# Second layer of a two-layer network on one core: all engines in source order, and the tile border reordered

## The chip, the cores and the metric

The kernel runs on 1 core of one Trainium2 chip. The metric is the device time of one execution in microseconds (us). The engines are named as in the profile: PE (TensorE), PEld (its weight loads), DVE (VectorE), ACT (ScalarE), POOL (GpSimd), SP (SyncE, which here only issues DMAs).

## The reference

An mLSTM-like attention over 4 batches, 8 heads, 768 steps and head size 40 gives 3072 tokens of 320 numbers. Two feed-forward layers follow, each 320 -> 2048 -> 320:

```
x  = attention(q, k, v, gates)             # 3072 x 320
x1 = square(max(x  @ w_in1, 0)) @ w_out1   # layer 0 in the code
h  = x1 @ w_in2                            # layer 1 in the code
g  = where(h > 0, h, exp(min(h, 0)) - 1)
out = g @ w_out2
```

All of it is float32. On PE each float32 operand is split into a high part (fp32r) and a rest, and three products high*high, high*low, low*high are added.

## The kernel before

Tokens are cut into 6 tiles of 512 (`NTILE`, `TT`), the hidden size of 2048 into 16 blocks of 128 (`NF`). `steps` lists (layer l, tile j, block m), step `k` being its index; the loop at L815 goes through them. The attention and the first steps are written out by hand (`ORDER`); the attention of later tiles is woven into the steps of layer 0. This change is about the second layer, l = 1, and the last two steps ahead of it.

In the second layer two blocks go together, so work is done at even `k`. `first_pair(k)` makes the hidden values of blocks m and m+1: 15 "slots" of two matmuls each, one on the lower 64 rows of the array and one on the upper 64 rows, into two PSUM tiles `h`. `elem(k)` and `elem(k+1)` make g from them: ACT `r` = relu(-h) (L520), `th` = tanh(r/2) (L521), `ex` = exp(-r) (L522); DVE two `scalar_tensor_tensor` (L523, L524); POOL the rounded `ghi` (L525). `elem_lo` is the rest `glo` on DVE (L530). `second_half(k)` multiplies half of the pair's rows into the four PSUM accumulators `acc0` to `acc3` (four groups of 128 tokens): 48 matmuls of 320 columns are needed for a pair, 24 in a first pass and 24 in a second pass ("again") with lower and upper rows exchanged. After a first pass `pass_banks` has ACT read one number of the accumulator written last into `mark` (the tile `room`, L615); the second pass waits for it.

The order on PE in the second layer is that of the source: in the step of pair k first `first_pair(k+2)`, then `second_half(k-2)` (second pass), then `second_half(k)` (first pass). So the elementwise work of a pair has the second passes and the first products of the next pair to hide behind.

At the border between tiles (m == 0, j > 0) the second pass of the old tile's last pair is followed by `put` (L626), which copies the four accumulators to SBUF (L639 on DVE) and stores them (L642 on SP). The copies go through `yp`, tag `y`, which has 3 buffers (`yp = pool("y", bufs=3)`, L86), so a fourth copy needs the buffer of the first. The new tile's `second_half(k)` then begins in the same four accumulators, one buffer each; at a border the passes work on `acc0` with `acc2` first, then on `acc1` with `acc3`.

PE alone has its source order there (`manual_schedule(engines={pe.engine})`, L819). ACT, DVE, POOL and SP are put in order by the scheduler of the framework, which estimates when each instruction will be ready. `behind(e)` only says that an instruction comes after the engine's last one traced so far.

Two side jobs run in the same loop. `y_split` (L653) cuts the next tile's input, read back from DRAM by `y_load`, into high and low parts, one of five slices at m = 2, 4, 6, 8, 10: ACT `hi` (L668), DVE `lo` (L669), and for the last slice (m = 10, c = 4) first a DVE addition `yr` (L667). In the source it stands ahead of the step's `pass_banks`. `w_next` prepares the second layer's weights block by block (L868 to L875): ACT `w_top` (L130) and `w_low` (L135), DVE `w_add` (L140), POOL `w_hi` (L144), DVE `w_lo` (L150). These steps run in the last tile of layer 0 and at even m of the second layer's first tile until 16 blocks are done.

Of the kernel before, what the change touches and what calls it, by code (L numbers as in the profile page):

```python
# [27 lines left out]
NF = DFF // 128  # L28
# [5 lines left out]
NTILE = NT // TT  # L34
# [29 lines left out]
def body(tc, qk, qp, kvo, gates, wq, ident_in, qkm_in, out):  # L64
    nc = tc.nc
    pe, act, dve, pool_, sp = nc.tensor, nc.scalar, nc.vector, nc.gpsimd, nc.sync
    es = ExitStack()

    def pool(name, bufs=1, stack=es, **kw):
        return stack.enter_context(tc.tile_pool(name=name, bufs=bufs, **kw))  # L70
# [372 lines left out]
    def attn_pe(t):  # L443
        u, k = divmod(t, 4)
        if k == 0:
            units(u, lambda u: [f() for f in scores(2 * u)])
        elif k == 1:
            units(u - 1, lambda w: [f() for f in trans(w)])
            units(u, lambda u: [f() for f in scores(2 * u + 1)])
        for c in range(1, NCH):  # L450
            if t == (16 * c - 9 if c > 1 else 9):
                for f in gate_cols(c):
                    f()
# [24 lines left out]
    def turn(t):  # L478
        for f in (attn_pre, attn_pe, attn_mul, attn_post, attn_last):
            f(t)  # L480

    G, HB, ACC = {}, {}, {}
# [45 lines left out]
    def elem_lo(k):  # L528
        hi, lo, r = G[k]
        dve.tensor_tensor(out=lo, in0=r, in1=hi.bitcast(F32), op=ALU.subtract)  # L530

    def acc_tile(i):
        return (pacc if i < 3 else bp["a"]).tile([128, 512], F32, tag=f"acc{i}", name=f"acc{i}")
# [34 lines left out]
    def first_pair(k):  # L568

        l, j, m, _ = steps[k]  # L570
        w = W[l, m]
        hi, lo = X[NTILE + j]
        ops = []
        for c in range(5):
            ws, wlo = (w[:, o + c * 128:o + c * 128 + 128] for o in (0, WC))
            ops += [(ws, hi[c]), (ws, lo[c]), (wlo, hi[c])]
        for i, t in enumerate((ph, bp["h"])):
            HB[k + i] = t.tile([128, TT], F32, tag="h", name="h")
        for n, (a, b_) in enumerate(ops):
            for i, r in enumerate((LOW, HIGH)):  # L580
                pe.matmul(HB[k + i], lhsT=a[r], rhs=b_[r], start=n == 0, stop=n == len(ops) - 1)  # L581

    def second_ops(k, i):

        l, j, m, _ = steps[k]
        w, cs, ops = W[l, m + 1], slice(i * L, (i + 1) * L), []
        for x in range(2):
            hi, lo, _ = G[k + x]
            wh, wl = (w[:, o + 384 * x:o + 384 * x + DM] for o in (0, WC))
            ops += [(hi[:, cs], wh), (hi[:, cs], wl), (lo[:, cs], wh)]  # L590
        return ops
# [4 lines left out]
    def second_half(k):  # L596

        l, j, m, _ = steps[k]
        if (l, j) not in ACC:
            ACC[l, j] = [acc_tile(i) for i in range(4)]  # L600
        again = k in begun
        begun.add(k)
        parts = [range(6)] if again else [(0, 1, 3, 4), (2, 5)]
        todo = []
        for own, r in zip(banks, (LOW, HIGH)):
            ops = {i: second_ops(k, i) for i in own}
            todo.append([(i, ops[i][n][0][r], ops[i][n][1][r], n) for part in parts for i in own for n in part])
        for pair in zip(*todo):
            for i, a, b_, n in pair:
                pe.matmul(ACC[l, j][i][:, 0:DM], lhsT=a, rhs=b_, start=m == 0 and not again and n == 0, stop=n == 5 and (not again or m + 2 == NF), skip_group_check=m > 0 or again)  # L610
# [15 lines left out]
    def put(k):  # L626
        l, j, m, _ = steps[k]
        if m < NF - 1:
            return
        for i, a in enumerate(ACC.pop((l, j))):  # L630
            if l == 0:
                t = yp.tile([128, TT], F32, tag="y", name="y")
                act.activation(out=t, in_=a, func=AF.Copy)
                sp.dma_start(out=y_dr[i, :, j * TT:(j + 1) * TT], in_=t)
            else:
                last = j == NTILE - 1
                t = (bp["t"].tile([128, TT], F32, tag="th", name="yl") if last and i == 3 else yp.tile([128, TT], F32, tag="y", name="y"))[:, 0:DM]
                if not last or i % 2:
                    dve.tensor_copy(t, a[:, 0:DM])  # L639
                else:  # L640
                    act.activation(out=t, in_=a[:, 0:DM], func=AF.Copy)
                (act if last and i % 2 else sp).dma_start(out=out[j * 4 + i], in_=t)  # L642
# [159 lines left out]
    def first(k):  # L802
        nonlocal nm
        todo = []
        while nm <= min(k, len(steps) - 1):
            for f in mm1(nm):
                f()
            todo.append(nm)
            nm += 1
        return todo  # L810

    def behind(e):
        return tc.issue_after(next(i for i in reversed(nc.cur_bb.bb.instructions) if i.engine == e.engine))

    for k in range(NK, len(steps)):  # L815
        l, j, m, _ = steps[k]
        if k == (NTILE - 1) * NF:
            early.close()
            es.enter_context(tc.manual_schedule(engines={pe.engine}))  # L819
            for e in (act, dve, pool_, sp):  # L820
                es.enter_context(behind(e))
        last = l == 0 and j == NTILE - 1
        ts = []
        if l == 0 and j + 1 < NTILE:
            to = 16 * j + m + 22
            ts = list(range(nt, min(TEND, to)))
            nt += len(ts)
        if last and m == 0:
            ea.close()
            bp["y"] = pool("by", reuse_waits="tile")  # L830
            bp["x"] = pool("bx", reuse_waits="tile")
            bp["t"] = pool("bt", bufs=2, reuse_waits="tile")
            bp["g"] = pool("bg", bufs=2, reuse_waits="tile")
            bp["a"] = pool("pa", space=PSUM, reuse_waits="tile")
            bp["h"] = pool("pb", bufs=2, space=PSUM, reuse_waits="tile")
        for t in ts[:-1]:
            turn(t)
        for t in ts[-1:]:
            attn_pre(t)
        if l or last and m > 13:  # L840
            todo = []
            if k % 2 == 0 and k + 2 < len(steps):
                first_pair(k + 2)
                todo = [k + 2, k + 3]
        else:
            todo = first(k + 2)
        for t in ts[-1:]:
            attn_pe(t)
        if l and j and m == 0:
            second_half(k - 2)  # L850
            put(k - 1)
        for e in todo:
            elem(e)
        for t in ts[-1:]:
            attn_mul(t)
        for e in todo:
            elem_lo(e)
        for t in ts[-1:]:
            attn_post(t)
        if l == 0 and j == 1 and 3 < m < 7:  # L860
            w_next(0, w_load)
        if l == 0 and 1 < j < NTILE - 1:
            if m == 5:
                w_next(1, w_top, w_low)
            if m == 8:
                w_next(2, w_add)
                w_next(0, w_load)
        if last or l == 1 and j == 0 and m % 2 == 0:  # L868
            if w_n[3] < min(w_n[2], NF + m if last else 2 * NF):
                w_next(3, w_hi, w_lo)  # L870
            if w_n[1] < min(w_n[0], NF + m if last else 2 * NF):
                w_next(1, w_top, w_low)
                w_next(2, w_add)
            if w_n[0] < min(w_n[2] + 3, 2 * NF):
                w_next(0, w_load)  # L875
        jn = j + 1 if l else 0
        if (l or last) and jn < NTILE:
            if m == 13 and jn + 1 < NTILE or last and m == 1:
                y_load(jn + (m > 1))
            if m in (2, 4, 6, 8, 10) if l else m in (4, 6, 8, 10, 12):  # L880
                with behind(act), behind(dve):
                    y_split(jn, (m - 2) // 2 if l else (m - 4) // 2)
        if l:
            if k % 2 == 0:
                if m and k < len(steps) - 2:
                    second_half(k - 2)
                if k < len(steps) - 4:
                    second_half(k)
                    pass_banks(j)
                elif k == len(steps) - 4:  # L890
                    second_whole(k)
            if k == len(steps) - 1:
                second_whole(k - 1)
                put(k)
            continue
        for f in mm2(k):
            f()
        put(k)
        for t in ts[-1:]:
            attn_last(t)  # L900
# [70 lines left out]
```

## Time and profile before

| | us |
|---|---|
| median of 3 runs | 840.22 |
| lowest, highest | 839.46, 840.56 |
| the profiled execution, its own time | 839.09 |
| its span, first to last instruction | 837.3 |
| PE busy | 802.4 |
| DVE busy | 531.9 |
| ACT busy | 513.4 |
| POOL busy | 158.0 |
| mean granted PE clock | 0.984 |

The profile is of one execution. The second layer's first products start at 454.77 us of the span and its last copy ends at 834.39 us. PE is busy nearly throughout, so what can be gained or lost lies in the short stretches where it waits or where its granted clock (1.0 is 2.4 GHz, 0.5 is 1.2 GHz) is low.

### The profile page before, as it was taken

Reading aid. Unit: us, or ns where it says so; the run is one execution under the profiler, and the core shown is the slowest. Engines: PE = TensorE matmul, PEld = TensorE weight load, DVE = VectorE, ACT = ScalarE, POOL = GpSimd, SP = SyncE. Lnnn points to the kernel's source line nnn. Section 1 sums busy time; section 2 is a strip of 40 time slices with the busy share of each in tenths; the row PEclk is TensorE's granted clock in tenths of the full one; section 3 lists DMA queues with packets and bytes.
Section 4 is the critical chain, followed back from the end, with each engine's and each line's share of the span. In section 5 each row is a group of like instructions: output and inputs, shape, how many; then the busy total and the mean of one; then the engine's idle time right before and its main releaser. Section 6 shows DMA issues by size and latency. Waiting matters only on the chain.

```text
span 837.3 us, 17781 instructions
## 1 busy us (share of the span) xinstructions
PE 802.4 (96%) x7058; PEld 701.3 (84%) x7058; DVE 531.9 (64%) x956; ACT 513.4 (61%) x1018; POOL 158.0 (19%) x209
## 2 busy tenths in 40 slices
PE   8999999999999999999999999898899799799798
PEld 5688788888888888888888898898898798798798
DVE  5899976866567665543486766565466466466454
ACT  5799776777768667774897655454354354354343
POOL 3233210100100000100122322122122122122121
PEclk9999999999999999999999999999899899999899
DMA  9997455757454455613256103003003003000000
GB/s 228 311 296 224 123 159 124 250 137 179 138 154 148 110 163 145 185 52 77 106 186 167 38 2 77 32 2 77 32 2 77 32 2 76 33 1 2 32 2 32
DMA packets 33257, 88.22 MB, mean 105 GB/s; under 512 B 3735, under 2 KB 7319, under 8 KB 33175
## 3 DMA queue, kind: packets, MB, share of 16 engines
q1 hardware_dynamic: 32887, 86.77, 37.1%
q8 instruction: 55, 0.90, 0.5%
q10 hardware_dynamic: 288, 0.33, 0.1%
q14 instruction: 27, 0.22, 0.1%
HBM read 78.35 MB, written 8.73 MB: 104 GB/s over the span
## 4 chain that ended last, share of the span: by engine, by line
PE 74%; DVE 12%; ACT 4%; DMA 4%; issue 4%; POOL 2%; SPq 1%; POOLq 0%; ACTq 0%; DVEq 0%
PE h L581 18%; PE acc L610 17%; PE acc L546 15%; PE h L501 15%; DVE w L150 2%; DVE ct L140 2%; PE pv L331 2%; DMA mb<-negm_dr 2%; DVE ex L523 2%; PE s L320 1%; PE in L331 1%; DVE glo L530 1%; DMA kvo<-kvo 1%; ACT ct L135 1%; DVE r L524 1%
## 5 line engine op out<-in xcount | busy, mean ns | idle before, releaser
L530 DVE TENSOR_TENSOR glo<-r,ghi 128x512 fp32r<-128x512 f32 x192 | 133.3, 695 | 111.3 <-ACT r L516 88.2
L501 PE MATMUL h<-xh,w 128*128 128x512 f32 x576 | 179.8, 394 | 0.0
L610 PE MATMUL acc<-w,ghi 64*128 64x320 f32 x1472 | 153.7, 314 | 26.2 <-POOL ghi L525 13.1
L610 PEld LDWEIGHTS acc<-w,ghi 64*128 64x128 f32 x1472 | 139.1, 190 | 31.7 <-POOL ghi L525 14.3
L523 DVE SCALAR_TENSOR_TENSOR ex<-ex,th 128x512 f32<-128x512 f32 x96 | 65.9, 687 | 122.1 <-ACT ex L522 122.0
L525 POOL TENSOR_SCALAR ghi<-r 128x512 fp32r<-128x512 f32 x96 | 86.6, 902 | 280.2 <-PE acc L610 149.8
L520 ACT ACTIVATE r<-h 128x512 f32<-128x512 f32 x96 | 52.1, 594 | 135.9 <-PE h L581 135.5
L501 PEld LDWEIGHTS h<-xh,w 128*128 128x128 f32 x576 | 108.1, 188 | 23.8
L546 PE MATMUL acc<-ghi,w 128*128 128x512 f32 x480 | 127.6, 395 | 0.0
L610 PE MATMUL acc<-w,glo 64*128 64x320 f32 x736 | 112.5, 313 | 0.0
L546 PEld LDWEIGHTS acc<-ghi,w 128*128 128x128 f32 x480 | 87.5, 188 | 17.4 <-ACT ct L135 0.4
L581 PE MATMUL h<-x,w 64*128 64x512 f32 x720 | 89.4, 393 | 0.0
L515 ACT ACTIVATE ghi<-r 128x512 fp32r<-128x512 f32 x96 | 60.6, 632 | 41.8 <-PE acc L546 40.5
L610 PEld LDWEIGHTS acc<-w,glo 64*128 64x128 f32 x736 | 85.7, 191 | 0.0
L581 PEld LDWEIGHTS h<-x,w 64*128 64x128 f32 x720 | 76.1, 187 | 7.2 <-issue 0.7
L546 PE MATMUL acc<-glo,w 128*128 128x512 f32 x288 | 81.8, 392 | 0.0
L514 ACT ACTIVATE r<-h 128x512 f32<-128x512 f32 x96 | 56.6, 589 | 39.1 <-PE h L501 37.7
L501 PE MATMUL h<-xl,w 128*128 128x512 f32 x192 | 74.9, 390 | 0.0
L524 DVE SCALAR_TENSOR_TENSOR r<-h,ex 128x512 f32<-128x512 f32 x96 | 66.3, 691 | 3.0
L546 PEld LDWEIGHTS acc<-glo,w 128*128 128x128 f32 x288 | 53.6, 188 | 11.3
L516 ACT ACTIVATE r<-r 128x512 f32<-128x512 f32 x96 | 60.8, 633 | 2.9
L521 ACT ACTIVATE th<-r 128x512 f32<-128x512 f32 x96 | 60.5, 630 | 0.0
(124 smaller groups left out, 1112.1 us busy)
## 6 DMA issues: line engine op xcount, KB each, us to landing
raw<-wq SPq DMA_DIRECT2D x32, 704.0 KB, 6.4
rqk<-qk SPq DMA_DIRECT2D x32, 480.0 KB, 7.9
kvo<-kvo SPq DMA_DIRECT2D x24, 488.0 KB, 5.4
mb<-negm_dr SPq DMA_DIRECT2D x40, 256.0 KB, 5.3
yr<-y_dr SPq DMA_DIRECT2D x12, 768.0 KB, 8.3
y_dr<-y SPq DMA_DIRECT2D x18, 256.0 KB, 3.6
qp<-qp SPq DMA_DIRECT2D x16, 256.0 KB, 6.2
out<-y SPq DMA_DIRECT2D x22, 160.0 KB, 1.8
```

The lines of the kernel that those rows point to most:

```text
L501: lambda i=i, a=a, b_=b_: pe.matmul(h[:, 0:n], lhsT=a, rhs=b_, start=(i == 0), stop=(i == len(seq) - 1))
L514: act.activation(out=r, in_=h, func=AF.Relu)
L515: act.activation(out=hi, in_=r, func=AF.Square)
L516: act.activation(out=r, in_=r, func=AF.Square)
L521: act.activation(out=th, in_=r, func=AF.Tanh, scale=0.5)
L523: dve.scalar_tensor_tensor(out=ex, in0=ex, scalar=1.0, in1=th, op0=ALU.add, op1=ALU.mult)
L524: dve.scalar_tensor_tensor(out=r, in0=h, scalar=0.0, in1=ex, op0=ALU.max, op1=ALU.subtract)
L525: pool_.tensor_scalar(out=hi, in0=r, scalar1=1.0, scalar2=1.0, op0=ALU.mult, op1=ALU.mult)
L530: dve.tensor_tensor(out=lo, in0=r, in1=hi.bitcast(F32), op=ALU.subtract)
L546: ops.append(lambda: pe.matmul(o, lhsT=l_, rhs=r_, start=first and st, stop=last and sp_))
L581: pe.matmul(HB[k + i], lhsT=a[r], rhs=b_[r], start=n == 0, stop=n == len(ops) - 1)
L610: pe.matmul(ACC[l, j][i][:, 0:DM], lhsT=a, rhs=b_, start=m == 0 and not again and n == 0, stop=n == 5 and (not again or m + 2 == NF), skip ...
```

## The change

From the last two steps of layer 0 on (`k == NTILE * NF - 2`), ACT, DVE, POOL and SP too keep the order of the source. `first_pair` returns its 15 slots as functions; in a border step 8 slots are issued, then the second pass of the old tile's last pair and `put`, then the other 7 slots, and only then the new pair's first pass. `put` copies accumulators 0 and 2 on DVE and 1 and 3 on ACT, in every tile of the second layer. `w_next` no longer runs in the last two steps of layer 0 nor at m = 0 of the second layer's first tile; the same calls happen later, at m = 2, 4, 6 and 8 of that tile. `y_split` in the second layer loses its `behind`, since its engines are in source order.

```diff
@@ first_pair
-        for n, (a, b_) in enumerate(ops):
+        h = HB[k], HB[k + 1]
+        def slot(n, a, b_):
             for i, r in enumerate((LOW, HIGH)):
-                pe.matmul(HB[k + i], lhsT=a[r], rhs=b_[r], start=n == 0, stop=n == len(ops) - 1)
+                pe.matmul(h[i], lhsT=a[r], rhs=b_[r], start=n == 0, stop=n == len(ops) - 1)
+        return [lambda n=n, o=o: slot(n, *o) for n, o in enumerate(ops)]
@@ put
-                if not last or i % 2:
+                if i % 2 == 0:
                     dve.tensor_copy(t, a[:, 0:DM])
                 else:
                     act.activation(out=t, in_=a[:, 0:DM], func=AF.Copy)
@@ the loop
+        if k == NTILE * NF - 2:
+            es.enter_context(tc.manual_schedule(engines={e.engine for e in (act, dve, pool_, sp)}))
...
-                first_pair(k + 2)
+                slots = first_pair(k + 2)
+                border = l and j and m == 0
+                for f in slots[:8 if border else 15]:
+                    f()
+                if border:
+                    second_half(k - 2)
+                    put(k - 1)
+                    for f in slots[8:]:
+                        f()
                 todo = [k + 2, k + 3]
...
-        if l and j and m == 0:
-            second_half(k - 2)
-            put(k - 1)
...
-        if last or l == 1 and j == 0 and m % 2 == 0:
+        if last and m < NF - 2 or l == 1 and j == 0 and m % 2 == 0 and m:
...
-                with behind(act), behind(dve):
+                with ExitStack() as st:
+                    if not l:
+                        for e in (act, dve):
+                            st.enter_context(behind(e))
                     y_split(jn, (m - 2) // 2 if l else (m - 4) // 2)
```

## Rows read from the trace of the kernel before

**Rows 1.** The page's head.
```profile
span 837.3 us, 17781 instructions
```
**Rows 2.** Waits, 440 to 838 us: total, times, longest.
```profile
PE acc L610 <- POOL ghi L525: 13.1, 5, 3.0
PE acc L610 <- DVE y L639: 8.9, 5, 3.1
PE acc L610 <- ACT room L615: 4.1, 4, 1.0
```
**Rows 3.** Timeline of PE, second border: start, us, instructions [idle before].
```profile
579.60 3.59 PE L581 MATMUL h<-x,w 64*128 64x512 f32 x30
583.03 0.45 PE L610 MATMUL acc<-w,ghi 64*128 64x320 f32 x4
...
587.94 0.38 PE L610 MATMUL acc<-w,ghi 64*128 64x320 f32 x1 [2.99 <-POOL ghi L525]
589.84 2.50 PE L610 MATMUL acc<-w,ghi 64*128 64x320 f32 x15 [1.52 <-DVE y L639]
...
592.95 5.16 PE L581 MATMUL h<-x,w 64*128 64x512 f32 x30
```
**Rows 4.** Timeline of the same border: DVE copy and SP store.
```profile
587.31 0.48 DVE L639 COPY y<-acc 128x320 f32<-128x320 f32 x1
...
587.82 2.91 SPq L642 DMA_DIRECT2D out<-y  x4
```
**Rows 5.** Windows: six undisturbed pair steps, then the five borders, two steps each.
```profile
475.98:517.62 41.64, 41.64 (x474) 37.96 (x471) 27.77 (x43) 21.77 (x47) 10.79 (x12) 1.00 0.18 38
517.62:536.53 18.91, 15.84 (x160) 14.91 (x158) 9.58 (x17) 6.80 (x15) 3.58 (x4) 0.91 0.12 40
...
579.60:601.33 21.73, 17.21 (x161) 16.14 (x158) 9.40 (x17) 6.80 (x15) 3.58 (x4) 0.84 0.09 32
644.40:666.13 21.73, 17.21 (x159) 16.14 (x157) 9.43 (x17) 6.80 (x15) 3.58 (x4) 0.84 0.09 31
709.21:729.39 20.18, 15.66 (x161) 14.58 (x158) 9.40 (x17) 6.80 (x15) 3.58 (x4) 0.92 0.09 33
772.46:793.36 20.90, 16.60 (x159) 15.41 (x157) 9.40 (x17) 6.64 (x14) 3.59 (x4) 0.84 0.09 33
```
**Rows 6.** DMA issues by tile: KB each, us to landing; then landings, 716 to 721 us.
```profile
out<-y SPq DMA_DIRECT2D x22, 160.0 KB, 1.8
...
DMA to landing us min/median/max: 1.8/2.8/4.0
```
**Rows 7.** Groups by line: ACT copies of accumulators.
```profile
L641 ACT ACTIVATE y<-acc 128x320 f32<-128x320 f32 x2 | 0.9, 438 | 5.1 <-PE acc L624 5.1
```
**Rows 8.** Timeline of the elementwise work of one undisturbed pair.
```profile
576.34 1.09 ACT L520 ACTIVATE r<-h 128x512 f32<-128x512 f32 x2 [3.32 <-PE h L581]
...
581.42 0.90 POOL L525 TENSOR_SCALAR ghi<-r 128x512 fp32r<-128x512 f32 x1 [0.43 <-DVE r L524]
...
582.35 0.69 DVE L530 TENSOR_TENSOR glo<-r,ghi 128x512 fp32r<-128x512 f32 x1 [0.51 <-POOL ghi L525]
```
**Rows 9.** Window of an m = 10 step, then such a step's timeline.
```profile
564.29:572.66 8.37, 7.34 (x83) 6.92 (x81) 5.74 (x10) 3.72 (x8) 1.84 (x3) 1.00 0.18 35
...
632.39 0.69 DVE L667 TENSOR_TENSOR yr<-yr 128x512 f32<-128x512 f32 x1
...
633.64 0.14 ACT L615 ACTIVATE room<-acc 1x1 f32<-1x1 f32 x1
```
**Rows 10.** Groups by line and form: weight work on DVE and POOL.
```profile
L140 DVE TENSOR_TENSOR ct<-ct,cu 128x704 uint16<-128x704 uint16 x32 | 33.3, 1043 | 12.4 <-ACT ct L135 12.3
L144 POOL TENSOR_SCALAR w<-ct 128x704 fp32r<-128x704 f32 x32 | 32.5, 1019 | 86.3 <-PE acc L546 56.4 <-DVE ct L140 19.7 <-ACT ct L135 3.6
L150 DVE TENSOR_TENSOR w<-ct,w 128x704 fp32r<-128x704 f32 x16 | 15.1, 942 | 3.3 <-POOL w L144 3.3
```
**Rows 11.** Timeline of PE at the start of the second layer.
```profile
467.47 1.15 PE L610 MATMUL acc<-w,ghi 64*128 64x320 f32 x12 [1.17 <-POOL ghi L525]
```

## The prediction, made before the changed kernel was run

> **What bounds the kernel now.** The page comes first: the span is 837.3 us [rows 1] and the PE is the busiest engine by far, so the time is the PE's work plus the stretches in which it waits or runs at half clock. The list of waits then says who keeps it waiting in the second layer: in all of 440 to 838 us there are only three releasers that matter [rows 2]. The reader is to see how few events these are: five, five and four. The timeline of the PE shows where the first two lie: at the tile borders. At the second border the first products of the new pair end near 583.03, the old pair's second pass follows, and then the PE waits 2.99 us and, after one matmul, 1.52 us more [rows 3].
>
> Whom it waits for is read by ends, not by the name given. POOL is named for the 2.99 us, but the first accumulator copy runs from 587.31 to 587.79 and the PE starts at 587.94 [rows 3, 4]. The next pass must begin in that accumulator, so the copy releases it; the second wait is put down to the copies already. The copies are late because DVE has them behind elementwise work of the next pair, although the second pass had ended near 584.8 (583.03 plus 1.75 us, the other half of the 6.94 us step). So the borders are bounded by the order on DVE. After the wait the 30 first products take 5.16 us in place of 3.59 [rows 3]: the granted clock falls to its lower level of 1.2 GHz, and the mean over the border's two steps is 0.84 [rows 5].
>
> What this costs is read from windows. Six undisturbed steps take 41.64 us, 6.94 each [rows 5]. The five borders, two steps each, take 18.91, 21.73, 21.73, 20.18 and 20.90; less 13.88 each that is 5.03, 7.85, 7.85, 6.30 and 7.02 us, in sum **34.05 us** over an undisturbed run, clock loss included.
>
> The third releaser, `room`, is a different place: the m = 10 steps of tiles 1 to 4, 8.37 us in place of 6.94 each [rows 9]; a row of one stands for four. There ACT's one-number read stands behind the cut of the last slice, which waits for DVE's `yr`.
>
> **The change, part by part.** *Border order.* The stall of 34.05 us goes if the copies are done when the new pass wants the accumulators. Take S as the start of a border step (579.60 in rows 3). 15 slots take 3.43 us (579.60 to 583.03), 0.229 each. So 8 slots and the second pass end at S + 1.83 + 1.75 = S + 3.58, the 7 other slots at S + 5.18; that is when `acc0` and `acc2` are wanted, and after 8 of the 24 matmuls, 0.58 us, at S + 5.76, `acc1` and `acc3`. DVE finishes the last `glo` of the pair made a step earlier: it starts 6.01 us after ACT's first `r` [rows 8], which ran 3.26 us ahead of S. In source order the copies are next on DVE, at S + 3.3 (0.6 us after that `glo` began, as the next independent DVE work follows here). Copy 0 ends at S + 3.8, copy 2 at S + 4.3: both before S + 5.18. Copy 1 on ACT (0.438 us, rows 7) starts when its accumulator is complete, about S + 3.8, and ends by S + 4.3. The wait for the copies goes.
>
> *What is late next is copy 3.* It has the buffer of copy 0 and must wait until that store has landed: 1.8 us from issue [rows 6], issued 0.03 us after the copy's end (587.79 to 587.82, rows 4). So copy 3 starts at about S + 3.8 + 1.9 = S + 5.7, ends at S + 6.15, and the PE follows at S + 6.25 (0.15 us from copy to PE, or a little less, as at 587.79 to 587.94). Wanted at S + 5.76: a stall of 0.49 us a border, **2.45 us** for five. The bounds are 0, if landing and copy are quicker by that much, and some 2.7 us a border, if it is the first store that takes 4.0 us [rows 6]. I take 0.49, from the median landing. No clock loss with it: with 1.03 us of waiting in the m = 10 steps the clock stayed at 1.00 [rows 9].
>
> By the Trainium skill, SBUF — State Buffer, section The DMA setup-cost knee, a transfer takes about 2 us plus its bytes at 436 GB/s; for a store of 160 KB that is an estimate of 2.4 us, and the stall would be 1.1 us a border and the sum 3 us longer. The trace's 1.8 us speaks against it for this store.
>
> Behind copy 3 on ACT stand both `elem` of the new pair. Their `r` would have started at S + 5.3 and starts at S + 6.1; the last high part is ready 5.98 us later (576.34 to 582.32, rows 8), at S + 12.1. The PE wants it after the next 15 slots and one second pass: S + 5.18 + 0.49 + 1.75 + 3.43 + 1.75 = S + 12.6. It fits by 0.5 us, so I cost it at nothing; without that cover each 0.1 us over it would be 0.1 us of the PE. DVE and SP are not held by copy 3: SP has only that store behind it.
>
> *Source order in ordinary steps.* ACT's order becomes r, th, ex for one block, then for the other, where now both r come first [rows 8]. The first block's `ex` comes a little earlier; the second can be later by at most one `r` that is waited for, about 0.6 us. The high part is then ready 6.0 to 6.6 us after the first `r`, and wanted 6.94 + 1.75 - 0.14 = 8.55 after it. It hides: 0. Should the elementwise chain lose this margin of 2 us, each step would pay.
>
> *m = 10.* `y_split` stands before `pass_banks` in the source, so ACT's read stays behind the cut: at 633.64, 1.25 us after `yr` began [rows 9]. The 4 x 1.43 us stay. In the first tile, which has no such loss now (its six steps of 6.94 are in rows 5), the read came ahead of the cut; in source order the loss appears there too: 1.43 us at least.
>
> *Weights.* The same `w_next` work moves to m = 2, 4, 6, 8 of the first tile. A call puts 0.94 + 1.04 us on DVE and 1.02 us on POOL [rows 10], and a slice's `lo` is in the same steps, so that DVE, with six elementwise operations of 0.69, is full for about 6.9 of 6.94 us with waits for POOL between. I estimate it falls behind by 0.4 to 1.3 us by m = 10. The products don't see that (margin above), but the m = 10 read does: the first tile loses 1.43 to 2.7 us; I take **2.2 us**. Above 2.7 us the clock might fall too, as it did after 2.99 us; what that costs is at most the 1.57 us of 5.16 less 3.59 [rows 3], so the upper end is 4.3.
>
> *Layer boundary.* With two steps fewer of that work on ACT, DVE and POOL, the wait of 1.17 us at 467.47 [rows 11] goes: **-1.17 us**, bounds 0 and -1.6 (the window from 462.29 to 469.04 can't be shorter than 15 slots and one pass, 5.18 us).
>
> *Tail.* DVE and ACT exchange copies; the last goes from a DVE copy to one of ACT, 0.438 us [rows 7] for 0.48 [rows 4]: 0.
>
> **The sum**, against the profiled execution's own time of 839.09 us: 839.09 - 34.05 + 2.45 + 2.2 - 1.17 = 808.5. The median of the runs shown is 840.22, 1.13 us above that execution; the forecast for a median is 808.5 + 1.13 = **809.6 us**.
>
> **The rivals.** *A: the copy wait is hidden after all.* The store of copy 0 lands sooner, or `acc3` is wanted later, so no border stalls, and the first tile's loss is the bare 1.43 us: 809.6 - 2.45 - 0.8 = 806.4, or 805 with the boundary's full gain. For it: 0.49 us is small. Against it: the buffer is the same one.
>
> *B: the border wait is only moved.* ACT waits on the slow landing of 4.0 us [rows 6], stands still for 2.7 us with both `elem` behind it, the PE loses that and, as after 2.99 us now, some clock, up to 1.5 us: 5 x (2.7 + 1.5 - 0.5) = 18 more, 828; with two borders of five so, 817. For it: landings of 4.0 us exist. Against it: the median is 1.8.
>
> *C: slower.* ACT in source order puts the one-number read behind every slice's cut and both `elem`. If that read, or the second block's high part, came after the PE's wish in every step, the PE would pay 46 times (48 pairs less the two at the ends). The break-even is 34 / 46 = 0.74 us a step; since the read is free about 3 us early in an ordinary step and the high part 2 us, the chain would have to be longer by 2.7 us than now. With 3 us longer, 1 us a step, it is 809.6 + 46 = 856. Against it: nothing on ACT grows by that.
>
> *D: it doesn't do what it says*, the copies still last in some border: 34.05 / 5 = 6.8 us each, 816 with one.
>
> **How the numbers follow.** Forecast 0.53 (805.5 to 813), A 0.2, B 0.13, D 0.07, C 0.05, and 0.02 for ending where it was. About 0.2% (1.7 us) is what a measurement can tell from no change here. Faster: the forecast, A, B and D, 0.93; same 0.02; slower 0.05. The range is 804 to 818: A and the forecast are in it, and of B and D the cases with one or two bad borders.
>
> **What would show it.** Right: the two steps of a border at 14 to 14.5 us, granted clock 1.00 throughout the second layer, the PE's only border wait about 0.5 us on ACT's copy 3, which starts some 1.9 us after copy 0's end; m = 10 steps of 8.4 us in tiles 1 to 4 and 9 us or so in tile 0; no wait at the layer boundary. Wrong: waits for POOL's high parts in ordinary steps, border steps over 16 us, or ordinary steps off 6.94.

## The result, and the profile after

The changed kernel takes 812.39 us in the median of 4 runs (811.3 to 815.33), the kernel before 839.97 us beside it: a ratio of 0.9677, 95% interval 0.965 to 0.9704. The forecast was 809.6 us, with a range of 804 to 818.

The profiled execution is the longest of the four, 815.33 us, and its span is 813.5 us, against 837.3 [rows 1]. The page's head:

```profile
span 813.5 us, 17783 instructions
```

Who the PE waits for in the second layer, from the list of waits (total, times, longest). Line numbers have moved: the matmuls of `second_half`, first and second passes alike, are L612 now, first products L582, the read L617, copies L641 on DVE and L643 on ACT, stores L644, `yr` L669:

```profile
ACT y L643 <- DMA out<-y: 9.8, 5, 2.0
PE acc L612 <- ACT room L617: 7.4, 5, 2.1
PE acc L612 <- ACT y L643: 2.9, 5, 0.6
```

The 13.1 and 8.9 us of [rows 2] have come down to 2.9, and the read's 4.1 us in four places have become 7.4 in five. The first line is new: ACT waits for a store, five times, once a border. The timeline of the second border, the PE first, which answers to [rows 3]:

```profile
580.16 2.00 PE L582 MATMUL h<-x,w 64*128 64x512 f32 x16
582.00 0.45 PE L612 MATMUL acc<-w,ghi 64*128 64x320 f32 x4
...
583.75 1.77 PE L582 MATMUL h<-x,w 64*128 64x512 f32 x14
585.36 0.89 PE L612 MATMUL acc<-w,ghi 64*128 64x320 f32 x9
...
586.83 0.85 PE L612 MATMUL acc<-w,ghi 64*128 64x320 f32 x7 [0.58 <-ACT y L643]
...
587.96 3.73 PE L582 MATMUL h<-x,w 64*128 64x512 f32 x30
```

and the other engines there, answering to [rows 4]:

```profile
583.31 0.69 DVE L530 TENSOR_TENSOR glo<-r,ghi 128x512 fp32r<-128x512 f32 x1 [0.52 <-POOL ghi L525]
...
583.92 0.88 DVE L641 COPY y<-acc 128x320 f32<-128x320 f32 x2
583.95 0.44 ACT L643 ACTIVATE y<-acc 128x320 f32<-128x320 f32 x1 [3.42 <-PE acc L612]
584.43 2.70 SPq L644 DMA_DIRECT2D out<-y  x4
586.34 0.44 ACT L643 ACTIVATE y<-acc 128x320 f32<-128x320 f32 x1 [1.95 <-DMA out<-y]
```

The reader sees 8 slots, the second pass, 7 slots, a third of the new pass and then one wait of 0.58 us. It ends when copy 3 ends on ACT, and copy 3 began when the store of copy 0, issued at 584.43, had landed 1.9 us later. The border step takes 7.80 us in place of 13.35. That is 0.86 us over an undisturbed step, more than the 0.58, because the list counts a wait only from the modelled end of the matmul before it.

An "m = 10 step" is named after the step whose cut and one-number read delay the PE. The passes that wait for that read are issued by the loop one step later, at m = 12. Windows (length, busy time of PE, PEld, DVE, ACT, POOL, then the granted clock) of the border step, the m = 10 steps of the first, second and third tile, and the step after the layer boundary:

```profile
580.16:587.96 7.80, 7.22 (x83) 6.33 (x80) 3.87 (x6) 2.38 (x7) 1.52 (x2) 1.00 0.22 80
...
504.16:515.02 10.86, 8.74 (x83) 7.79 (x80) 8.25 (x13) 4.08 (x9) 2.42 (x3) 0.84 0.28 64
...
564.44:573.22 8.78, 7.34 (x83) 6.92 (x81) 6.05 (x9) 4.09 (x9) 1.91 (x3) 1.00 0.17 39
622.66:631.05 8.39, 7.35 (x83) 6.93 (x81) 5.67 (x9) 4.09 (x9) 2.23 (x3) 1.00 0.17 44
...
464.15:469.46 5.31, 5.31 (x55) 4.67 (x56) 2.79 (x4) 2.76 (x6) 1.17 (x2) 1.00 0.39 150
```

Step by step, taken from the starts of the first products, the difference of the two profiled executions is:

| stretch | before | after | difference |
|---|---|---|---|
| ahead of the second layer | 454.77 | 456.63 | +1.86 |
| step after the layer boundary | 6.75 | 5.31 | -1.44 |
| five borders, over undisturbed steps | 34.05 | 4.33 | -29.72 |
| m = 10 step, first tile, over 6.94 | 0 | 3.92 | +3.92 |
| m = 10 steps, tiles 1 to 4, over 6.94 each | 5.73 | 6.96 | +1.23 |
| rest (tail, rounding) | | | +0.39 |
| own time | 839.09 | 815.33 | -23.76 |

The first line is not the change's: the code there is the same. All of it is there before the first products of the first layer, which start at 37.7 us in place of 35.8. The PE waited 1.93 us near the start, in place of 1.04 before, and then the granted clock stood at 0.50 from 20 to 25 us:

```profile
17.89 0.75 PE L389 MATMUL in<-ident,xt 128*128 128x128 f32 x3 [1.93 <-DVE xt L380]
...
20.00:25.00 5.00, 5.00 (x66) 4.38 (x66) 2.95 (x6) 2.23 (x5) 1.00 (x2) 0.50 1.02 241
```

In the execution before it was 1.00 in the same 5 us. Two of the four executions of the changed kernel have a mean clock of 1.0 and take 811.3 and 811.89 us.

One more thing is new, in ordinary steps. The timeline of POOL and DVE (start, duration) in the m = 10 step of the second tile:

```profile
564.54 0.62 POOL L525 TENSOR_SCALAR ghi<-r 128x512 fp32r<-128x512 f32 x1 [3.97 <-DVE r L524]
564.61 1.08 DVE L523 SCALAR_TENSOR_TENSOR ex<-ex,th 128x512 f32<-128x512 f32 x1 [0.25 <-ACT ex L522]
```

L523 takes 0.69 us everywhere before. Here it begins 0.07 us after POOL's operation and takes 0.4 us more, while POOL takes 0.62 in place of 0.90 [rows 8]. The groups of L523, before and after (busy us, then the mean in ns):

```profile
L523 DVE SCALAR_TENSOR_TENSOR ex<-ex,th 128x512 f32<-128x512 f32 x96 | 65.9, 687 | 122.1 <-ACT ex L522 122.0
...
L523 DVE SCALAR_TENSOR_TENSOR ex<-ex,th 128x512 f32<-128x512 f32 x96 | 81.3, 846 | 79.0 <-ACT ex L522 78.1 <-ACT room L617 0.8
```

### The profile page after: what moved, and what is told of

Read it like the earlier page. It is cut to its first block, busy times and chain, and to the rows that moved or that the text cites. A ratio compares the mean times of both kernels' runs of the same rounds, so it can differ in the third digit from the quotient of the medians.

```text
span 813.5 us, 17783 instructions
## 1 busy us (share of the span) xinstructions
PE 794.0 (98%) x7054; PEld 694.2 (85%) x7058; DVE 548.0 (67%) x946; ACT 526.3 (65%) x1028; POOL 146.2 (18%) x209
## 4 chain that ended last, share of the span: by engine, by line
PE 79%; DVE 10%; ACT 3%; issue 3%; DMA 2%; POOL 2%; SPq 1%; POOLq 0%; ACTq 0%; DVEq 0%
PE acc L546 19%; PE h L501 19%; PE acc L612 16%; PE h L582 16%; PE pv L331 2%; PE s L320 2%; PE in L331 2%; DVE glo L530 2%; DVE w L150 2%; DVE ex L523 1%; DVE ct L140 1%; DMA kvo<-kvo 1%; DVE r L524 1%; DMA out<-y 1%; POOL ghi L525 1%
## 5 line engine op out<-in xcount | busy, mean ns | idle before, releaser
L530 DVE TENSOR_TENSOR glo<-r,ghi 128x512 fp32r<-128x512 f32 x192 | 135.7, 707 | 118.9 <-ACT r L516 93.8
L612 PE MATMUL acc<-w,ghi 64*128 64x320 f32 x1472 | 149.6, 309 | 10.4 <-ACT room L617 7.4
L612 PEld LDWEIGHTS acc<-w,ghi 64*128 64x128 f32 x1472 | 136.3, 186 | 15.4 <-ACT room L617 9.6
L523 DVE SCALAR_TENSOR_TENSOR ex<-ex,th 128x512 f32<-128x512 f32 x96 | 81.3, 846 | 79.0 <-ACT ex L522 78.1
L525 POOL TENSOR_SCALAR ghi<-r 128x512 fp32r<-128x512 f32 x96 | 76.5, 797 | 277.2 <-DVE r L524 242.9
L520 ACT ACTIVATE r<-h 128x512 f32<-128x512 f32 x96 | 56.4, 588 | 100.5 <-PE h L582 100.5
L612 PE MATMUL acc<-w,glo 64*128 64x320 f32 x736 | 109.4, 307 | 0.0
L582 PE MATMUL h<-x,w 64*128 64x512 f32 x720 | 88.3, 388 | 0.0
L514 ACT ACTIVATE r<-h 128x512 f32<-128x512 f32 x96 | 56.6, 590 | 42.5 <-PE h L501 41.2
L612 PEld LDWEIGHTS acc<-w,glo 64*128 64x128 f32 x736 | 81.6, 185 | 0.0
L582 PEld LDWEIGHTS h<-x,w 64*128 64x128 f32 x720 | 74.4, 184 | 7.1 <-issue 0.7
```

The costliest lines, as they stand in the source:

```text
L514: act.activation(out=r, in_=h, func=AF.Relu)
L523: dve.scalar_tensor_tensor(out=ex, in0=ex, scalar=1.0, in1=th, op0=ALU.add, op1=ALU.mult)
L525: pool_.tensor_scalar(out=hi, in0=r, scalar1=1.0, scalar2=1.0, op0=ALU.mult, op1=ALU.mult)
L582: pe.matmul(h[i], lhsT=a[r], rhs=b_[r], start=n == 0, stop=n == len(ops) - 1)
```

## The experiments

Theory at this point: the border's loss was the copies' place in the queues; source order on top of it keeps two losses of its own, the read behind the cut and copy 3's buffer. The rivals stand in each expectation. Each ratio is against the kernel before, on the same chip.

**Source order without the split.**
```diff
-                for f in slots[:8 if border else 15]:
+                for f in slots:
                     f()
                 if border:
                     second_half(k - 2)
                     put(k - 1)
-                    for f in slots[8:]:
-                        f()
```


> The changed kernel with the border step in the old order: all 15 slots of first products, then the old pair's second pass and the copies, then the new pair's first pass. Source order on all engines stays. Theory (the copies' place in the engines' queues is what the border lost): the copies still come ahead of the next pair's elementwise work, so most of the gain stays; the passes now meet the copies with no slots between, copy 3 starts about 1.9 us after copy 0 at S + 6.9, and a border step takes about 9 us in place of 7.8: 818 us in all (816 to 821). Rival (the 7 slots between are what hides the copies): the borders lose 5 to 7 us each again, 838 us or more.

Measured: 818.27 us, ratio 0.9731 (0.9704 to 0.9758). Four border steps take 8.57 to 8.64 us; the last takes 9.84, with a longer wait and the granted clock at 0.57 from 762 to 764 us. The PE at the second border and at the last:

```profile
584.97 0.84 PE L612 MATMUL acc<-w,ghi 64*128 64x320 f32 x7 [1.12 <-ACT y L643]
...
762.11 1.32 PE L612 MATMUL acc<-w,ghi 64*128 64x320 f32 x7 [1.56 <-ACT y L643]
```

The wait at the second border is copy 3's, twice as long as with the split. So the change without its split brings most of the gain: source order, with the copies shared with ACT and the weight work moved.

**The split without source order.** The kernel before, with these edits of the change alone (and `first_pair` returning its slots):
```diff
-                first_pair(k + 2)
+                slots = first_pair(k + 2)
+                border = l and j and m == 0
+                for f in slots[:8 if border else 15]:
+                    f()
+                if border:
+                    second_half(k - 2)
+                    put(k - 1)
+                    for f in slots[8:]:
+                        f()
...
-        if l and j and m == 0:
-            second_half(k - 2)
-            put(k - 1)
```


> The kernel before with the border step of the change (8 slots, second pass, copies, 7 slots) and nothing else of it: ACT, DVE, POOL and SP stay in the scheduler's order, all copies on DVE. Theory: with the 7 slots behind the copies, the next pair's elementwise work becomes ready later, so the scheduler too puts the copies first, and either half of the change would do most of it: 811 to 818 us, border steps of 7.5 to 9 us. Rival (only the source order gets the copies ahead): the copies stay behind elementwise work, 830 to 840 us.

Measured: **801.9 us**, ratio 0.9537 (0.9514 to 0.956): better than the whole change, whose interval begins at 0.965, and below the range of the theory's expectation. The timeline of its second border, without the PE:

```profile
575.77 0.69 DVE L530 TENSOR_TENSOR glo<-r,ghi 128x512 fp32r<-128x512 f32 x1 [0.52 <-POOL ghi L525]
576.38 1.35 DVE L641 COPY y<-acc 128x320 f32<-128x320 f32 x3
576.89 2.74 SPq L644 DMA_DIRECT2D out<-y  x4
...
578.78 0.49 DVE L641 COPY y<-acc 128x320 f32<-128x320 f32 x1 [1.04 <-DMA out<-y]
```

The scheduler itself now puts the copies directly behind `glo`. Only copy 3 waits for the store; the border steps take 7.43 to 7.78 us. And the m = 10 steps take 6.94 us in every tile. ACT there:

```profile
559.48 0.16 ACT L617 ACTIVATE room<-acc 1x1 f32<-1x1 f32 x1 [0.50 <-PE acc L612]
563.16 0.63 ACT L670 ACTIVATE x<-yr 128x512 fp32r<-128x512 f32 x1 [3.52 <-DVE yr L669]
```

The read stands ahead of the cut, where before the scheduler had it behind in tiles 1 to 4 [rows 9]. The split moved that choice too; the source was the same. What is left here is the layer boundary: 7.39 us for the step that takes 5.31 with the whole change.

**Copy 3 in another buffer.**
```diff
-                t = (bp["t"].tile([128, TT], F32, tag="th", name="yl") if last and i == 3 else yp.tile(...))[:, 0:DM]
+                t = (bp["t"].tile([128, TT], F32, tag="th", name="yl") if i == 3 else yp.tile(...))[:, 0:DM]
```


> The changed kernel with copy 3 of every tile in a buffer of its own (tag th, as the last tile has it) and no longer in copy 0's. Theory: the 0.55 to 0.62 us of waiting at each border are copy 3 waiting for copy 0's store to land; without it the border steps fall from 7.8 to 6.94 us and the time by 4.3 us, to about 808. Rival (the ACT copy itself is late, or the accumulator is): the border steps stay at 7.8 us, 812.

Measured: 810.04 us, ratio 0.9638 (0.9612 to 0.9665). The five border steps take 6.96 us: the wait was the buffer. But the step after the border takes 8.21 us in tile 4 and 7.94 in tile 5, the others 6.94. The timeline behind the fourth border:

```profile
695.38 0.40 SPq L644 DMA_DIRECT2D out<-yl  x1
...
699.58 0.63 ACT L521 ACTIVATE th<-r 128x512 f32<-128x512 f32 x1 [2.15 <-DMA out<-yl]
```

`th` needed the tile and could start only 4.2 us after the store's issue. The loss moved from the copy to `th` where a landing was slow; some 2 to 3 of the expected 4.3 us are left of the gain, and the intervals of the two ratios overlap, so the gain itself is read from the steps.

**The read ahead of the cut.**
```diff
                     second_half(k)
                     pass_banks(j)
+                    if jn < NTILE and m in (2, 4, 6, 8, 10):
+                        y_split(jn, (m - 2) // 2)
```
(and `y_split` for l = 1 no longer at its old place)

> The changed kernel with the cut of the next tile's input traced behind the step's one-number read of ACT, not ahead of it. Theory: the losses of the m = 10 steps (3.9 us in the first tile, 1.45 to 1.84 in the four others, 10.9 us in all) are that read standing behind the cut's wait for DVE; they go, every m = 10 step takes 6.94 us, and the time falls to about 801.5 us. Rival (DVE is what is full there, so the wait comes back in the next step as late high parts): 809 or more, with waits for POOL's high parts after m = 10.

Measured: 803.47 us, ratio 0.9558 (0.9533 to 0.9584), 2 us above the expected 801.5. Every m = 10 step takes 6.94 us, in the first tile too. The PE's list of waits in the second layer has one line left, the copies':

```profile
PE acc L612 <- ACT y L643: 3.0, 5, 0.6
```

**Both r of a pair first on ACT.** `elem` is divided into `elem_r` (the tiles and `r`) and `elem_g` (`th`, `ex` and what follows).
```diff
         for e in todo:
-            elem(e)
+            elem_r(e)
+        for e in todo:
+            elem_g(e)
```


> The changed kernel with both r of a pair ahead of its th and ex on ACT, as the scheduler had them before. Theory: in the changed kernel the second block's DVE operation L523 starts just after POOL's ghi has begun and waits for it (1.09 us in place of 0.69); with both r first, DVE starts first, L523's mean falls from 846 to about 690 ns, POOL's ghi goes from 797 to about 900 ns, the m = 10 steps of tiles 1 to 4 come to 8.39 us each, and the copies at the borders start 0.4 us earlier, so that a border step takes 7.4 us in place of 7.8: about 3.5 us less, 809 us. Rival (L523 is long for a reason of its own, as ACT's tiles): L523 stays at 846 ns and the time at 812.

Measured: 808.15 us, ratio 0.962 (0.9589 to 0.9651). The groups of its page (L535 is what L523 was, L537 what L525 was):

```profile
L537 POOL TENSOR_SCALAR ghi<-r 128x512 fp32r<-128x512 f32 x96 | 86.2, 898 | 262.4 <-DVE r L536 151.7 <-PE acc L624 94.3 <-PE acc L558 13.8
...
L535 DVE SCALAR_TENSOR_TENSOR ex<-ex,th 128x512 f32<-128x512 f32 x96 | 65.9, 687 | 92.4 <-ACT ex L534 92.4
```

DVE is back at 687 ns and POOL at 898; m = 10 steps of tiles 1 to 4 take 8.37 to 8.38 us, the first tile's 8.92, borders 7.39 to 7.71. So whichever of the two engines comes second pays, and which one that is follows from ACT's order.

**The weight steps where they were.**
```diff
-        if last and m < NF - 2 or l == 1 and j == 0 and m % 2 == 0 and m:
+        if last or l == 1 and j == 0 and m % 2 == 0:
```


> The changed kernel with the weight steps where they were: in the last two steps of layer 0 and from m = 0 of the first tile. Theory: the step after the layer boundary takes 6.7 us or more again in place of 5.31 (a loss of 1.4), and the first tile's m = 10 step takes 8.4 to 8.8 us in place of 9.3 to 10.9, with no clock loss, for DVE is no longer behind (a gain of 0.5 to 2): 811 to 813 us. Rival (the first tile's extra loss has another cause than the weight work): the m = 10 step stays at 9.3 us or more and the time goes to 814.

Measured: 813.48 us, ratio 0.9678 (0.9647 to 0.9708), the same as the change's and 0.5 us above the range expected. The first tile's m = 10 step takes 8.78 us, like tile 1's, so its extra 0.5 us (9.3 in two of the kernels above) came from the weight work on DVE. Whether the clock loss did too is not shown: those two kernels have the same weight work and lost no clock there. The two steps at the layer boundary take 5.90 and 7.99 us in place of 5.31 and 6.94. So moving this work gains 1.64 us at the boundary, and at m = 10 it loses 0.52, or 2.08 where the clock falls as well. As a whole it brought nothing that the medians can tell.

**The read first, and copy 3 in a free buffer.** The edit of the read above, and
```diff
-                t = (bp["t"].tile([128, TT], F32, tag="th", name="yl") if last and i == 3 else yp.tile(...))[:, 0:DM]
+                t = (cvt.tile([128, TT], F32, tag="ct", name="yl") if i == 3 else yp.tile(...))[:, 0:DM]
```


> The changed kernel with the cut behind the one-number read and with copy 3 in a buffer that nothing else uses by then (tag ct, of the weight work). Theory: both losses go without the store's landing reaching anything: border steps 6.96 us, m = 10 steps 6.94, no step with a wait, 803.5 - 4.3 = 799.2 us. Rival (the landing matters elsewhere too, as it did for the tile th): 801 or more, single steps of 7.5 to 8.2 us after a border.

Measured: **797.98 us**, ratio 0.9491 (0.9464 to 0.9519), the fastest median. Two windows hold the second layer from its second step to near its end; the PE is busy in all of both, at full clock:

```profile
467.27:515.85 48.58, 48.58 (x550) 44.30 (x548) 41.75 (x57) 33.02 (x64) 14.83 (x18) 1.00 0.13 29
515.85:786.00 270.15, 270.15 (x3029) 245.92 (x3026) 191.25 (x269) 151.32 (x303) 59.60 (x78) 1.00 0.13 32
```

Its L523 still takes 868 ns in the mean; in these windows the PE never waits for it.

**The split alone, and copy 3 in the free buffer.** The edit of the buffer above on the kernel with the split alone.

> The kernel before with the border step of the change, in the scheduler's order, and copy 3 in a buffer of its own (tag ct). Theory: its border steps of 7.44 to 7.78 us also wait for copy 0's store alone and fall to 6.95: 801.9 - 2.8 = 799.1 us, with the wait at the layer boundary left (7.39 us for that step, against 5.31 in source order). Rival (the scheduler, with other releases, places the copies or the read elsewhere): 803 or more.

Measured: 799.9 us, ratio 0.9511 (0.9482 to 0.954). The borders take 6.95 to 6.96 us, the layer boundary 6.48 with 0.90 us of waiting for POOL. The intervals of the last two overlap, so which is faster is not settled. The boundary speaks for the one in source order (5.31 against 6.48 us), the last stretch, from the last first products on, for the other (12.77 against 12.36).

## Why the prediction was right, point by point

*The border.* Right in place and mechanism. The copies' place was the loss, copy 3's buffer the remainder, and it starts 1.9 us after copy 0's end. Its size was off: 0.84 to 0.90 us a border for 0.49. The step that was mis-sized is the start of copy 0. It was put at S + 3.3, since DVE would be free there; it was at S + 3.76 (583.92), because `glo` ran 0.4 us late behind the longer L523. The kernel with both `r` first on ACT bears this out: with L523 at 0.69 us its copy 0 starts at S + 3.36 to 3.37, and three borders take 7.39 to 7.41 us, 0.45 to 0.47 over an undisturbed step. In its other two (7.59 and 7.71 us) copy 3 starts 2.1 and 2.2 us after the store's issue, in place of 1.9. "Nothing on ACT grows" was true, but the new order on ACT made DVE's operation meet POOL's.

*Behind copy 3.* Costed at nothing, and nothing was seen: the steps after the borders take 6.94 to 6.95 us.

*Source order in ordinary steps.* Costed at nothing in ordinary steps: right, 6.94 us each. In the m = 10 steps of tiles 1, 3 and 4 (8.77 and 8.78 us; tile 2 has 8.39, and there DVE came first) the same 0.4 us of L523 reached the PE: +1.23 us in all that the sum lacked.

*The first tile's m = 10 step.* The mechanism held, and the weight work behind it was shown by its removal. Its size was off: 3.92 us for 2.2. Of that, 9.30 - 6.94 = 2.36 us is the wait (the two kernels with the same wait and no clock loss), and 1.56 us is clock. That the 2.36 is so near the 2.2 is in part luck. Beside the read's 1.43 us, the weight work cost 0.52 (9.30 less 8.78) where 0.8 was put, and the longer L523 cost 0.4 (9.30 less 8.92) where nothing was. The clock loss stood at the upper end of the term, tied to a loss above 2.7 us; it came after a wait of 2.12.

*The layer boundary*: -1.44 for -1.17. *The tail* was put at 0 and is +0.39 at most: the last pair's `glo` is late too, and the weight load of the last pass waits 0.36 us for it.

*The median.* The forecast added 1.13 us to its own sum, as the profiled execution before was short. The one after was long, by 2.9 us against its median: 1.86 us arose at the start and 1.56 is the clock at m = 10. The forecast is 2.8 us below the median measured, about what the borders (1.88) and the other m = 10 steps (1.23) take more than the sum had, less 0.27 at the layer boundary; the clock losses come and go from run to run.

*The signs.* Two steps of a border take 14.72 to 14.79 us, just over the 14 to 14.5 that were named; three of the four later m = 10 steps take 8.8 us for 8.4, and the clock was not 1.00 throughout. None of the signs of being wrong appeared. One of the sums is off: rival A with the boundary's full gain comes to 806, not 805 (806.4 less 0.43).

*What the prediction had wrong without its number showing it* is the part that source order plays. It said that the borders are bounded by the order on DVE and took the change's source order as what mends it, with no look at what the scheduler would do once the second pass stands between the slots. The split alone mends it, and the rest of the change (source order, the copies shared with ACT, the moved weight work) adds some 10 to 12 us (0.9677 against 0.9537 of the time before): the read goes behind the cut in all five tiles (10.9 us in the profile, 1.56 of it clock), four of the borders are 0.4 us longer, and only the layer boundary gains, 2.1. Sharing the copies with ACT was not tried by itself. The rival B was half seen, in the kernel with copy 3 in `th`, where two slow landings, the longer of 4.2 us, reached ACT.

By the Trainium skill, SBUF — State Buffer, section The DMA setup-cost knee, the stall would have been 1.1 us a border (an estimate). The measured wait of 1.9 us from issue to ACT's start speaks for the trace's 1.8 us; the excess had the other cause. The Trainium skill, SBUF — State Buffer, section Who interferes with whom, says that a DVE instruction with two SBUF inputs contends with a GpSimd instruction that reads SBUF, and that the order of issue decides who is blocked. The runs agree: L523 at 1.08 us with POOL at 0.62 when POOL is first, 0.69 and 0.90 when DVE is.

## What to carry to other kernels

Before an order is fixed by hand, test the reordering that it is meant to protect alone: a scheduler that put work badly for one program may put it well once the work between two users of a buffer is longer. A small instruction on which the bottleneck engine waits, like the one-number read here, has to stand ahead of everything in its queue that waits for another engine. Where a copy shares a buffer with a store that has just been issued, count the store's landing; the buffer of a job that is long finished is free.

## What was not expected of the hardware

The granted clock fell to its lower level after a wait of 2.12 us in the profiled execution of the change (0.50 from 511 to 513 us), and at the kernel's start after one of 1.93 us. In the kernel without the split it fell after a wait of 1.56 us, at its last border (0.57 from 762 to 764 us). Yet the first tile's m = 10 step has waits of 2.09 and 2.10 us and no fall in the kernel without the split and in the one with copy 3 in `th` (steps of 9.30 and 9.31 us, clock 1.00). Nor did the clock fall after 1.82 us at the layer boundary of the split alone, or after 1.56 us at m = 10 with the weight steps where they were. So the length of a wait does not by itself tell whether the clock falls: from 1.56 to 2.12 us it came out either way. Where it fell at m = 10, it cost 1.56 us (10.86 less 9.30).

A store of 160 KB landed in 1.8 us in the median, but the four behind the fourth border of the kernel with copy 3 in `th` took 1.8 to 4.4 us, with a median of 4.2. Why they were slow there is open.
